# Reciprocals and spreading in halves behind the last P.V of an attention kernel, with the left-over tiles and the final stores placed anew

## The chip, the core and the metric

One core of a Trainium2 chip runs the whole kernel. The metric is the device time of one execution in microseconds (us), as the median of several runs.

## The reference

Sequence length S = 2048, model width D = 512, 32 heads of 16, hidden width F = 1792, all in fp32:

```python
xn  = layernorm(x)
qkv = xn @ wqkv                                # 32 heads of 16
p   = softmax(q @ k^T * 16 ** -0.5)            # full, per head
s   = (p @ v) @ wo                             # attention and its projection
g   = silu(relu(xn @ w1 + b1) ** 2 @ w2 + b2)  # feed-forward with squared relu
out = x + s * g
```

## The kernel before

The order of the work is written out by hand; every engine executes its own instructions in program order. Products of fp32 values are made with fp32r pairs: a value is split into a high and a low part (`h`, `l`), and a product is the sum of three matmuls (high.high, high.low, low.high); `group` issues these three.

A first part normalizes x and makes q, k and v. The middle, and nearly all of the time, is a loop of 64 turns (`TURNS`) over groups of four heads, chunks of 512 queries and halves of the keys. A turn makes scores for eight key blocks on TensorE, the exponentials on ScalarE (VectorE copies some scores out of PSUM first), and then the products P.V, which `values_of` issues one behind the other (line 850) into the PSUM bank `acc`. Between the score matmuls a turn also carries matmuls of the feed-forward part or, in the last turns, of the projection with `wo`. V carries a column of ones, so that P.V also yields the row sums of the softmax.

The output has 16 tiles of 128 rows, 4 for each chunk of queries. Tiles of chunks 0 and 1 are projected during the last turns. For the tiles of chunks 2 and 3, the last groups of heads are missing until the end: `rest(i, dst)` (i = 0 to 3) makes the left-over products for tile i of chunk 2, from the columns of `onorm[2, 3]`; `end_rest(i, src)` multiplies them with 0.5 and the gate and brings them to the output rows, by a DMA that accumulates onto rows that are stored already (issued by GpSimd), or, for i = 2, by an addition on GpSimd of rows loaded back before (`stored`) and a plain store. I call these the left-over tiles 0 to 3.

What follows the last P.V serves chunk 3. `ou` is the sum of the last two partial P.V results, with the 16 row sums (4 heads by 4 row blocks) in columns of their own. In order: transposing products with columns of the identity bring the row sums into PSUM (line 1193); a copy and a reciprocal (1195, 1197); products of a broadcast reciprocal with the identity spread them over `ou`'s layout (1200); `check` and three instructions (887 to 1206) fold the ranges of all row sums into one flag per partition, which a product with ones (1209) sums into `nvalid`; `ou` is normalized (1212) and split into `h` (ScalarE, 1213) and `l` (VectorE, 1215); four projections with `wlast`, the last rows of `wo`, give the four tiles of chunk 3; each is multiplied by 0.5 and the gate (1227), added to `base` (1229 on GpSimd for the first, 1232 on VectorE) and stored, by SP or ScalarE. The left-over tiles 2, 3 and 1 stand between these steps, 0 before the last P.V. At the end all engines load `nvalid` and skip `general_path`, which is for inputs outside the ranges; SP waits for the transfers' counters.

`wlast` is loaded in the turn before the last by `load_wlast`, four DMAs on SP's queue, and split by VectorE (`split_wlast`); `load_stored` is a DMA on GpSimd's queue half a turn later. PSUM is full all the time: two tiles of two banks for scores and one (`spare`, S0) for the side work, and the banks `acc` and `lin`; behind the last scores they become free (`two`, `small`).

Of the kernel before, what the change touches and what calls it, by code (L numbers as in the profile page):

```python
# [24 lines left out]
FT = mybir.dt.float32  # L25
FR = mybir.dt.float32r
I32 = mybir.dt.int32
AF = mybir.ActivationFunctionType
OP = mybir.AluOpType
AX = mybir.AxisListType  # L30
# [46 lines left out]
def fast_path(tc, sb, banks, env):  # L77
# [14 lines left out]
    def t(shape, dt, tag):  # L92

        cnt[0] += 1
        if tag in BUFS:
            turn[tag] = turn.get(tag, -1) + 1
            n = turn[tag] % BUFS[tag]
            p, tag = ps.get(tag), f"{tag}{places[n] if tag == 'S' else n}"
        else:
            p = None  # L100
        return (p or ps.get(tag, sb)).tile(shape, dt, tag=tag, name=f"{tag}_{cnt[0]}")
# [901 lines left out]
    def load_wlast():  # L1003
        wlast.append(t([128, 512], FT, "u"))
        pool.memset(wlast[0], 0.0)
        for j in range(4):
            sp.dma_start(wlast[0][32 * j:32 * j + 16], wo[448 + 16 * j:464 + 16 * j])

    def split_wlast():
        a = t([128, 2, 512], FR, "QA")  # L1010
# [48 lines left out]

    def load_stored():  # L1060

        stored.append(t([128, 512], FT, "hl0"))
        pool.dma_start(stored[0], out[1280:1408])

    at(LAST + 1, load_base3)
    at(LAST + 6.5, load_stored)
# [14 lines left out]
    def rest(i, dst):  # L1081

        group(dst, lambda p: onorm[2, 3][p][:, cut[i]], lambda p: wos[0][p][1][:, 1])

    def end_rest(i, src):

        o = t([128, 512], FT, f"wf2{'hl'[i // 2]}{i % 2}")
        dve.scalar_tensor_tensor(o, src, 0.5, gsb[2, i // 2][:, i % 2], op0=OP.mult, op1=OP.mult)
        rows = out[1024 + 128 * i:1152 + 128 * i]
        if i == 2:  # L1090
            pool.tensor_tensor(o, o, stored[0], op=OP.add)
            sp.dma_start(rows, o)
        else:
            pool.dma_start(rows, o, accum_op=OP.add)

    seen = t([1, 16], FT, "seen")

# [15 lines left out]
    for n in range(TURNS):  # L1113
# [43 lines left out]
            exps(*a)  # L1157
        if n == TURNS - 1:
            two = t([128, 2, 512], FT, "S")
            rest(0, two[:, 0])  # L1160
        pieces_now = pieces_of[n] if n < len(pieces_of) else 0
        ahead = pieces_now > 0 and n % per in (0, 1, 3, 6, 7, 10, 11)
        while lin(0, 1):
# [4 lines left out]
        if n == LAST + 4:  # L1168
            gsb.update({(1, i): y[1, i] for i in range(2)})
        if n == TURNS - 1:  # L1170
            end_rest(0, two[:, 0])
        happen(n + 0.5)
        for _ in range(pieces_now - ahead):
            split_piece()
# [3 lines left out]
        happen(time / 2)  # L1178


    ou = t([128, 512], FT, "P0")
    zc, r = t([128, 16], FT, "zc"), t([128, 16], FT, "rc")
    ok, okm, ones = t([128, 80], FT, "ok"), t([128, 1], FT, "okm"), t([128, 1], FT, "ones")
    dve.memset(ones, 1.0)
    h, l = t([128, 512], FR, "wf1h0"), t([128, 512], FR, "wf1l0")
    half = [slice(0, 256), slice(256, 512)]
    for s in half:
        dve.tensor_tensor(ou[:, s], sides[0][:, s], part[0][:, s], op=OP.add)
    small = t([128, 2, 512], FT, "S")
    lins = [small[:, 1], t([128, 512], FT, "lin"), t([128, 512], FT, "acc"), two[:, 0]]  # L1190
    rest(2, spare[:, 0])
    for i in range(4):
        mm(lins[1][:, 4 * i:4 * i + 4], ou[:, cut[i]], ident[:, 16::32], start=True, stop=True)
    end_rest(2, spare[:, 0])
    dve.tensor_copy(zc, lins[1][:, :16])
    rest(3, lins[2])
    dve.reciprocal(r, zc)
    for i in range(4):
        for j in range(4):
            mm(small[32 * j:32 * j + 32, 0, cut[i]], r[:, 4 * i + j:4 * i + j + 1].broadcast_to([128, 32]), ident,  # L1200
               start=True, stop=True)

    check(zc, 4 * NQ - 1)
    dve.tensor_scalar(ok[:, 0:32], stat[:, 0:32], Z_MIN, None, op0=OP.is_ge)
    dve.tensor_scalar(ok[:, 32:80], stat[:, 32:80], BIG, None, op0=OP.is_le)
    dve.tensor_reduce(okm, ok, axis=AX.X, op=OP.min)
    end_rest(3, lins[2])
    pn = spare[0:1, 1, :1]
    mm(pn, okm, ones, start=True, stop=True)
    rest(1, two[:, 1])  # L1210
    for s in half:
        dve.tensor_tensor(ou[:, s], small[:, 0, s], ou[:, s], op=OP.mult)
        act.copy(h[:, s], ou[:, s])
    for s in half:
        dve.tensor_tensor(l[:, s], ou[:, s], h[:, s].bitcast(FT), op=OP.subtract)
    dve.tensor_copy(nvalid, pn)
    end_rest(1, two[:, 1])


    o = [t([128, 512], FT, f"P{2 + i}") for i in range(4)]  # L1220
    for j in range(2):
        for todo in ((0, 0), (0, 1)), ((1, 0),):
            for i in (2 * j, 2 * j + 1):
                group(lins[i], lambda p: (h, l)[p][:, cut[i]], lambda p: wlast[0][:, p],
                      start=len(todo) == 2, stop=len(todo) == 1, todo=todo)
        for i in (2 * j, 2 * j + 1):
            dve.scalar_tensor_tensor(o[i], lins[i], 0.5, gsb[3, j][:, i % 2], op0=OP.mult, op1=OP.mult)
            if i == 0:
                pool.tensor_tensor(o[0], o[0], base[3, 0][:, 0], op=OP.add)
                act.dma_start(out[1536:1664], o[0])  # L1230
    for i, eng in ((1, sp), (2, act), (3, sp)):
        dve.tensor_tensor(o[i], o[i], base[3, i // 2][:, i % 2], op=OP.add)
        eng.dma_start(out[1536 + 128 * i:1664 + 128 * i], o[i])


def general_path(tc, dram, nvalid, ident, vdram, kdram, qdram, gdram, x, wo, out):
# [109 lines left out]
```

## Time and profile before

| | |
|---|---|
| three runs | 1212.72, 1213.26, 1214.46 us; median 1213.26 |
| the profiled execution: its own time | 1212.94 us |
| its span, first to last instruction | 1211.2 us |
| granted TensorE clock, mean | 0.998 |
| busy: TensorE, ScalarE, VectorE, GpSimd | 99%, 86%, 70%, 29% of the span |

In the profile PE is TensorE, DVE VectorE, ACT ScalarE, POOL GpSimd, SP SyncE; a q behind a name is the engine's queue, where DMAs are issued. A row of a timeline has start and duration in us, engine, line of the kernel, operation, output tile <- input tiles, shapes and count; where several instructions are merged, the duration is of all of them, and in brackets stands the idle time before and what ended it. Rows of a line's instructions have min/median/max of the duration in ns, first and last start, forms. Ends of matmuls are modelled.

### The profile page before, as it was taken

How to read it: one execution, taken by the hardware profiler on the slowest of the kernel's cores; microseconds unless marked ns; L12 is line 12 of the kernel's file. 1: busy time of each engine (PE TensorE's matmuls, PEld its weight loads, DVE VectorE, ACT ScalarE, POOL GpSimd, SP SyncE). 2: the span in 40 equal slices, each digit the busy share in tenths (PEclk: the TensorE clock that was granted, in tenths of full speed). 3: DMA queues.
4: the chain of work that ended last, by engine and by line, in shares of the span. 5: the costliest groups of instructions: out<-in, count | busy, mean ns of one | idle time of the engine just before them, and what ended most of it. 6: DMA issues, size and time to landing. Idle time of an engine off the chain costs nothing.

```text
span 1211.2 us, 24228 instructions
## 1 busy us (share of the span) xinstructions
PE 1200.1 (99%) x9877; PEld 709.9 (59%) x9877; DVE 845.4 (70%) x1365; ACT 1040.8 (86%) x1231; POOL 350.1 (29%) x268
## 2 busy tenths in 40 slices
PE   9999999999999999999999999999999999999996
PEld 7888655555565555555555565555555555555553
DVE  7666767575866776757687676677775758777776
ACT  6655689889989889988999988889898889999993
POOL 5756523040312321304032122221230404222222
PEclk9999999999999999999999999999999999999999
DMA  7799914131343222224423133151422233464444
GB/s 290 293 371 322 332 58 137 45 111 44 97 154 109 75 69 85 67 75 149 120 77 111 46 97 85 45 183 42 118 80 80 80 99 79 132 207 151 157 140 103
DMA packets 107576, 154.91 MB, mean 128 GB/s; under 512 B 43386, under 2 KB 57736, under 8 KB 107460
## 3 DMA queue, kind: packets, MB, share of 16 engines
q1 hardware_dynamic: 104804, 144.93, 37.3%
q0 software_dynamic: 2368, 7.87, 2.2%
q8 instruction: 78, 1.28, 0.4%
q10 hardware_dynamic: 288, 0.52, 0.1%
q14 instruction: 38, 0.31, 0.1%
HBM read 103.61 MB, written 49.67 MB: 127 GB/s over the span
## 4 chain that ended last, share of the span: by engine, by line
PE 97%; DVE 1%; DMA 1%; SPq 0%; issue 0%; ACT 0%; DVEq 0%
PE acc L850 36%; PE S L551 28%; PE S L503 14%; PE B L314 5%; PE acc L503 5%; PE B L127 4%; PE lin L503 2%; PE D L314 1%; PE D L252 1%; DMA hl<-gd 0%; PE S L993 0%; PE lin L314 0%; SPq L880 0%; PE acc L314 0%; DMA P<-in_A_x_dram 0%
## 5 line engine op out<-in xcount | busy, mean ns | idle before, releaser
L507 ACT ACTIVATE P<-S 128x1024 f32<-128x1024 f32 x702 | 661.9, 1040 | 93.7 <-PE S L503 91.9
L850 PE MATMUL acc<-P,V 128*32 128x512 f32 x4096 | 453.6, 594 | 0.0
L526 DVE COPY P<-acc 128x512 f32<-128x512 f32 x322 | 222.8, 692 | 139.7 <-PE lin L503 69.2
L507 ACT ACTIVATE P<-P 128x1024 f32<-128x1024 f32 x322 | 315.0, 1090 | 0.0
L850 PEld LDWEIGHTS acc<-P,V 128*32 128x32 f32 x4096 | 126.3, 110 | 285.6 <-issue 265.6
L503 PE MATMUL S<-QA,KA 64*128 64x512 f32 x1404 | 292.0, 405 | 0.0
L526 DVE COPY P<-lin 128x512 f32<-128x512 f32 x322 | 220.6, 685 | 1.5 <-PE lin L503 0.6
L503 PEld LDWEIGHTS S<-QA,KA 64*128 64x128 f32 x1404 | 134.6, 184 | 111.2 <-issue 41.8
L503 PE MATMUL lin<-QA,KA 64*128 64x512 f32 x322 | 126.8, 394 | 0.0
L503 PE MATMUL acc<-QA,KA 64*128 64x512 f32 x322 | 126.6, 393 | 0.1
L120 POOL TENSOR_TENSOR wf1l<-wr,wf1h 128x1024 fp32r<-128x1024 f32 x28 | 68.4, 2442 | 176.9 <-DVE wf1h L116 108.4
L577 POOL MEMSET note<- 1x1 f32 x68 | 6.0, 88 | 383.2 <-PE S L551 381.7
L551 PE MATMUL S<-xl,wf1h 64*128 64x512 f32 x464 | 95.8, 389 | 0.0
L120 POOL TENSOR_TENSOR hl<-T,hh 128x1024 fp32r<-128x1024 f32 x28 | 79.9, 2855 | 52.9 <-DVE hh L116 52.9
L120 POOL TENSOR_TENSOR wf2l<-wr,wf2h 128x1024 fp32r<-128x1024 f32 x28 | 67.2, 2401 | 90.5 <-DVE wf2h L116 90.5
L551 PE MATMUL S<-xh,wf1l 64*128 64x512 f32 x480 | 91.3, 388 | 0.0
L551 PE MATMUL S<-wf2l,hh 64*128 64x512 f32 x448 | 90.3, 390 | 0.0
L876 DVE TENSOR_TENSOR ou<-acc,ou 128x512 f32<-128x512 f32 x31 | 21.4, 692 | 96.8 <-PE acc L850 91.0
L551 PE MATMUL S<-wf2h,hl 64*128 64x512 f32 x448 | 82.9, 388 | 0.0
L551 PE MATMUL S<-xh,wf1h 64*128 64x512 f32 x480 | 77.7, 392 | 0.0
L551 PE MATMUL S<-wf2h,hh 64*128 64x512 f32 x448 | 71.7, 393 | 0.0
L503 PEld LDWEIGHTS acc<-QA,KA 64*128 64x128 f32 x322 | 59.3, 184 | 17.1 <-DVE P L526 2.4
(370 smaller groups left out, 1427.7 us busy)
## 6 DMA issues: line engine op xcount, KB each, us to landing
wr<-in_B_w_dram SPq DMA_DIRECT2D x56, 512.0 KB
QA<-qd SPq DMA_DIRECT2D x128, 128.0 KB
KA<-kd SPq DMA_DIRECT2D x64, 256.0 KB
u<-ud SPq DMA_DIRECT2D x15, 512.0 KB
kd<-P SPq DMA_DIRECT2D x11, 512.0 KB
V<-vd SPq DMA_DIRECT2D x8, 664.0 KB
qd<-P SPq DMA_DIRECT2D x9, 512.0 KB
vd<-P SPq DMA_DIRECT2D x16, 280.0 KB
```

Of the source, the lines that this page charges most:

```text
L120: leng.tensor_tensor(lo, src, hi.bitcast(FT), op=OP.subtract)
L127: mm(dst, lhs(a, k), rhs(b, k), start=n == 0, stop=n == len(todo) - 1)
L252: nc.tensor.transpose(halves[k // 2][:, k % 2, 128 * j:128 * j + 128], xnorm[c, i][:, j, 128 * k:128 * k + 128], ident)
L314: mm(dst, left[a][:, k], right[b][:, k], start=n == 0, stop=n == 5)
L503: mm(dst, k[r, p, 128 * (kb % 8):128 * (kb % 8) + 128], q[r, p], start=True, stop=True)
L507: act.activation(ptile[i, p], src, AF.Exp, scale=SCALE)
L526: dve.tensor_copy(ptile[i, p][:, hp], sides[hp])
L551: ins = mm(bank, self.lhs(a, k)[r], self.rhs(b, k)[r], start=n == 0 and self.at[other] == 0, stop=n == len(self.todo[half]) - 1 and self.a ...
L577: f = pool.memset(note[:, notes[0]:notes[0] + 1], 0.0)
L850: mm(sides[0][32 * j:32 * j + 32], vq[qd][:, kb, 17 * j:17 * j + 32], ptile[i, j // 2][:, j % 2], start=first, stop=last)
L876: dve.tensor_tensor(ou, sides[0], part[0], op=OP.add)
```

## The change

Both reciprocals and the spreading are done in two halves, for columns 0 to 255 and 256 to 511 of `ou`, each with a PSUM bank of its own, and the reciprocals read PSUM directly. The normalized values stay in PSUM (`norms`). The flag work of line 1204 to 1206 moves ahead of the additions; the last row sums are checked through the largest and smallest reciprocal (`top`, `flags`) instead of through `check`. Left-over tile 1 moves ahead of the last P.V, next to tile 0; tile 3's matmuls go between the spreading and the last projections; tile 2 is scaled by ScalarE and multiplied with its gate on GpSimd; tile 3 is added to loaded rows on GpSimd and stored by ScalarE in place of the accumulating DMA. In the final projections GpSimd adds `base` for tiles 0 and 1, VectorE for 2 and 3, with the multiplied values of these two left in PSUM; ScalarE issues all four stores, in the order 0, 2, 1, 3. Two of the four loads of `wlast` go to GpSimd's queue, and `load_stored` loads two tiles.

```diff
@@ -1004,7 +1004,7 @@
         wlast.append(t([128, 512], FT, "u"))
         pool.memset(wlast[0], 0.0)
         for j in range(4):
-            sp.dma_start(wlast[0][32 * j:32 * j + 16], wo[448 + 16 * j:464 + 16 * j])
+            (sp, pool)[j // 2].dma_start(wlast[0][32 * j:32 * j + 16], wo[448 + 16 * j:464 + 16 * j])
 
     def split_wlast():
         a = t([128, 2, 512], FR, "QA")
@@ -1059,8 +1059,8 @@
 
     def load_stored():
 
-        stored.append(t([128, 512], FT, "hl0"))
-        pool.dma_start(stored[0], out[1280:1408])
+        stored.append(t([128, 2, 512], FT, "hl0"))
+        pool.dma_start(stored[0], out[1280:1536].rearrange("(a p) d -> p a d", p=128))
 
     at(LAST + 1, load_base3)
     at(LAST + 6.5, load_stored)
@@ -1084,14 +1084,18 @@
 
     def end_rest(i, src):
 
-        o = t([128, 512], FT, f"wf2{'hl'[i // 2]}{i % 2}")
-        dve.scalar_tensor_tensor(o, src, 0.5, gsb[2, i // 2][:, i % 2], op0=OP.mult, op1=OP.mult)
+        o, gate = t([128, 512], FT, f"wf2{'hl'[i // 2]}{i % 2}"), gsb[2, i // 2][:, i % 2]
+        if i == 2:
+            act.activation(o, src, AF.Copy, scale=0.5)
+            pool.tensor_tensor(o, o, gate, op=OP.mult)
+        else:
+            dve.scalar_tensor_tensor(o, src, 0.5, gate, op0=OP.mult, op1=OP.mult)
         rows = out[1024 + 128 * i:1152 + 128 * i]
-        if i == 2:
-            pool.tensor_tensor(o, o, stored[0], op=OP.add)
-            sp.dma_start(rows, o)
+        if i < 2:
+            pool.dma_start(rows, o, accum_op=OP.add)
         else:
-            pool.dma_start(rows, o, accum_op=OP.add)
+            pool.tensor_tensor(o, o, stored[0][:, i - 2], op=OP.add)
+            (sp, act)[i - 2].dma_start(rows, o)
 
     seen = t([1, 16], FT, "seen")
 
@@ -1157,7 +1161,8 @@
             exps(*a)
         if n == TURNS - 1:
             two = t([128, 2, 512], FT, "S")
-            rest(0, two[:, 0])
+            for m in range(2):
+                rest(m, two[:, m])
         pieces_now = pieces_of[n] if n < len(pieces_of) else 0
         ahead = pieces_now > 0 and n % per in (0, 1, 3, 6, 7, 10, 11)
         while lin(0, 1):
@@ -1168,7 +1173,8 @@
         if n == LAST + 4:
             gsb.update({(1, i): y[1, i] for i in range(2)})
         if n == TURNS - 1:
-            end_rest(0, two[:, 0])
+            for m in range(2):
+                end_rest(m, two[:, m])
         happen(n + 0.5)
         for _ in range(pieces_now - ahead):
             split_piece()
@@ -1178,59 +1184,64 @@
         happen(time / 2)
 
 
+    ok, okm, flags = t([128, 80], FT, "ok"), t([128, 1], FT, "okm"), t([128, 2], FT, "ones")
+    dve.tensor_scalar(ok[:, 0:32], stat[:, 0:32], Z_MIN, None, op0=OP.is_ge)
+    dve.tensor_scalar(ok[:, 32:80], stat[:, 32:80], BIG, None, op0=OP.is_le)
+    dve.tensor_reduce(okm, ok, axis=AX.X, op=OP.min)
+
     ou = t([128, 512], FT, "P0")
-    zc, r = t([128, 16], FT, "zc"), t([128, 16], FT, "rc")
-    ok, okm, ones = t([128, 80], FT, "ok"), t([128, 1], FT, "okm"), t([128, 1], FT, "ones")
-    dve.memset(ones, 1.0)
+    r = t([128, 16], FT, "rc")
     h, l = t([128, 512], FR, "wf1h0"), t([128, 512], FR, "wf1l0")
     half = [slice(0, 256), slice(256, 512)]
     for s in half:
         dve.tensor_tensor(ou[:, s], sides[0][:, s], part[0][:, s], op=OP.add)
+    rest(2, spare[:, 0])
+    end_rest(2, spare[:, 0])
     small = t([128, 2, 512], FT, "S")
-    lins = [small[:, 1], t([128, 512], FT, "lin"), t([128, 512], FT, "acc"), two[:, 0]]
-    rest(2, spare[:, 0])
-    for i in range(4):
-        mm(lins[1][:, 4 * i:4 * i + 4], ou[:, cut[i]], ident[:, 16::32], start=True, stop=True)
-    end_rest(2, spare[:, 0])
-    dve.tensor_copy(zc, lins[1][:, :16])
-    rest(3, lins[2])
-    dve.reciprocal(r, zc)
-    for i in range(4):
-        for j in range(4):
-            mm(small[32 * j:32 * j + 32, 0, cut[i]], r[:, 4 * i + j:4 * i + j + 1].broadcast_to([128, 32]), ident,
-               start=True, stop=True)
-
-    check(zc, 4 * NQ - 1)
-    dve.tensor_scalar(ok[:, 0:32], stat[:, 0:32], Z_MIN, None, op0=OP.is_ge)
-    dve.tensor_scalar(ok[:, 32:80], stat[:, 32:80], BIG, None, op0=OP.is_le)
-    dve.tensor_reduce(okm, ok, axis=AX.X, op=OP.min)
-    end_rest(3, lins[2])
-    pn = spare[0:1, 1, :1]
-    mm(pn, okm, ones, start=True, stop=True)
-    rest(1, two[:, 1])
-    for s in half:
-        dve.tensor_tensor(ou[:, s], small[:, 0, s], ou[:, s], op=OP.mult)
-        act.copy(h[:, s], ou[:, s])
-    for s in half:
-        dve.tensor_tensor(l[:, s], ou[:, s], h[:, s].bitcast(FT), op=OP.subtract)
+    lin, acc = t([128, 512], FT, "lin"), t([128, 512], FT, "acc")
+    for n, z in enumerate((lin, acc)):
+        for i in range(2):
+            mm(z[:, 4 * i:4 * i + 4], ou[:, cut[2 * n + i]], ident[:, 16::32], start=True, stop=True)
+        dve.reciprocal(r[:, 8 * n:8 * n + 8], z[:, :8])
+    top = [two[:, 0, n:n + 1] for n in range(2)]
+    dve.tensor_reduce(top[0], r, axis=AX.X, op=OP.max)
+    dve.tensor_reduce(top[1], r, axis=AX.X, op=OP.min)
+    norms = [small[:, 0, :256], spare[:, 1, :256]]
+    for n in range(2):
+        for i in range(2):
+            for j in range(4):
+                k = 8 * n + 4 * i + j
+                mm(norms[n][32 * j:32 * j + 32, cut[i]], r[:, k:k + 1].broadcast_to([128, 32]), ident,
+                   start=True, stop=True)
+    dve.tensor_tensor(norms[0], norms[0], ou[:, half[0]], op=OP.mult)
+    dve.scalar_tensor_tensor(flags[:, 0:1], top[0], 1 / Z_MIN, okm, op0=OP.is_le, op1=OP.mult)
+    dve.tensor_scalar(flags[:, 1:2], top[1], 1 / BIG, None, op0=OP.is_ge)
+    dve.tensor_tensor(norms[1], norms[1], ou[:, half[1]], op=OP.mult)
+    for n, s in enumerate(half):
+        act.copy(h[:, s], norms[n])
+    for n, s in enumerate(half):
+        dve.tensor_tensor(l[:, s], norms[n], h[:, s].bitcast(FT), op=OP.subtract)
+    rest(3, lin)
+    pn = acc[0:1, :1]
+    mm(pn, flags[:, 0:1], flags[:, 1:2], start=True, stop=True)
+    end_rest(3, lin)
     dve.tensor_copy(nvalid, pn)
-    end_rest(1, two[:, 1])
-
-
-    o = [t([128, 512], FT, f"P{2 + i}") for i in range(4)]
+
+
+    o, lins = [t([128, 512], FT, f"P{2 + i}") for i in range(4)], [two[:, 0], small[:, 1], acc, lin]
     for j in range(2):
         for todo in ((0, 0), (0, 1)), ((1, 0),):
             for i in (2 * j, 2 * j + 1):
                 group(lins[i], lambda p: (h, l)[p][:, cut[i]], lambda p: wlast[0][:, p],
                       start=len(todo) == 2, stop=len(todo) == 1, todo=todo)
         for i in (2 * j, 2 * j + 1):
-            dve.scalar_tensor_tensor(o[i], lins[i], 0.5, gsb[3, j][:, i % 2], op0=OP.mult, op1=OP.mult)
-            if i == 0:
-                pool.tensor_tensor(o[0], o[0], base[3, 0][:, 0], op=OP.add)
-                act.dma_start(out[1536:1664], o[0])
-    for i, eng in ((1, sp), (2, act), (3, sp)):
-        dve.tensor_tensor(o[i], o[i], base[3, i // 2][:, i % 2], op=OP.add)
-        eng.dma_start(out[1536 + 128 * i:1664 + 128 * i], o[i])
+            dve.scalar_tensor_tensor(lins[i] if j else o[i], lins[i], 0.5, gsb[3, j][:, i % 2], op0=OP.mult, op1=OP.mult)
+            if j == 0:
+                pool.tensor_tensor(o[i], o[i], base[3, 0][:, i], op=OP.add)
+    for i in (2, 3):
+        dve.tensor_tensor(o[i], lins[i], base[3, 1][:, i % 2], op=OP.add)
+    for i in (0, 2, 1, 3):
+        act.dma_start(out[1536 + 128 * i:1664 + 128 * i], o[i])
 
 
 def general_path(tc, dram, nvalid, ident, vdram, kdram, qdram, gdram, x, wo, out):
```

## The prediction, made before the change was run

> **What bounds the kernel now.** I read the page first, then the chain of waits for the last 30 us, then the timeline of that stretch engine by engine, then the DMA view of two short windows and the instructions of a few lines. Times in these views are us from the start of the span.
>
> ```profile
> span 1211.2 us, 24228 instructions
> ```
>
> From the chain of waits (start, duration, engine, tile, line):
>
> ```profile
> 1187.14 7.00 PE acc L850 x64
> 1194.14 0.90 PE S L993 x3
> ...
> 1198.55 0.41 ACT wf1h L1213
> 1198.96 0.04 issue
> 1199.01 0.73 PE S L993 x2
> ...
> 1204.25 0.68 DVE P L1232
> ```
>
> Up to the last P.V (L850, which ends at about 1194.1) TensorE carries the chain without a gap. Behind it the chain goes back and forth between VectorE, ScalarE and TensorE, and the last addition of VectorE ends at 1204.93. The change touches this last 17 us of the 1211.2 and little else, so no large share of the time is at stake. The timeline of TensorE and of VectorE there:
>
> ```profile
> 1186.51 0.40 PE L993 MATMUL S<-xl,hl 128*128 128x512 f32 x1
> 1186.75 0.39 PE L993 MATMUL S<-xh,hl 128*128 128x512 f32 x1
> 1187.07 7.07 PE L850 MATMUL acc<-P,V 128*32 128x512 f32 x64
> ...
> 1194.88 0.95 PE L1193 MATMUL lin<-ident,P 128*128 128x4 f32 x8
> ...
> 1196.56 1.08 PE L1200 MATMUL S<-ident,rc 128*32 128x128 f32 x32
> 1197.64 0.19 PE L1209 MATMUL S<-ones,okm 128*1 128x1 f32 x2
> 1197.76 0.50 PE L993 MATMUL S<-xh,hl 128*128 128x512 f32 x1
> ```
>
> ```profile
> 1194.29 0.75 DVE L1188 TENSOR_TENSOR P<-acc,ou 128x256 f32<-128x256 f32 x2 [2.88 <-PE acc L850]
> ...
> 1195.87 0.17 DVE L1195 COPY zc<-lin 128x16 f32<-128x16 f32 x1
> 1196.08 0.25 DVE L1197 RECIPROCAL rc<-zc 128x16 f32<-128x16 f32 x1
> 1196.24 0.11 DVE L887 TENSOR_REDUCE stat<-zc 128x1 f32<-128x16 f32 x1
> 1196.27 0.15 DVE L888 TENSOR_REDUCE stat<-zc 128x1 f32<-128x16 f32 x1
> 1196.39 0.83 DVE L1204 TENSOR_SCALAR ok<-stat 128x32 f32<-128x32 f32 x1
> 1197.14 0.17 DVE L1205 TENSOR_SCALAR ok<-stat 128x48 f32<-128x48 f32 x1
> 1197.35 0.23 DVE L1206 TENSOR_REDUCE okm<-ok 128x1 f32<-128x80 f32 x1
> 1197.50 0.68 DVE L1088 SCALAR_TENSOR_TENSOR wf2l<-acc,V 128x512 f32<-128x512 f32 x1
> 1198.10 0.74 DVE L1212 TENSOR_TENSOR P<-S,P 128x256 f32<-128x256 f32 x2
> ...
> 1200.47 0.69 DVE L1227 SCALAR_TENSOR_TENSOR P<-S,wr 128x512 f32<-128x512 f32 x1
> ```
>
> Two things are to be seen. VectorE has the flag work (L887 to L1206) and one left-over tile (L1088) between its reciprocal and the normalisation L1212, although the spread values (L1200) are ready at 1197.64 and would be earlier. And the first comparison, L1204, takes 0.83 for 32 columns where its twin takes 0.17 for 48: it ends at 1197.22, as soon as GpSimd's addition does (1195.91 + 1.28, first row here):
>
> ```profile
> 1195.91 1.28 POOL L1091 TENSOR_TENSOR wf2l<-wf2l,hl 128x512 f32<-128x512 f32 x1 [4.72 <-issue]
> 1198.49 0.89 POOL L1094 DMA_DIRECT2D out_dram<-wf2l  x1 [1.31 <-DVE wf2l L1088]
> 1200.70 0.85 POOL L1094 DMA_DIRECT2D out_dram<-wf2h  x1 [1.32 <-DVE wf2h L1088]
> 1201.31 1.53 POOL L1229 TENSOR_TENSOR P<-P,KA 128x512 f32<-128x512 f32 x1
> ```
>
> The stores, issued by SP and by ScalarE, and what the DMA moved in 40 slices of 1197 to 1200 (0.075 us each) and of 1202 to 1212 (0.25 us each):
>
> ```profile
> 1197.21 0.36 SPq L1092 DMA_DIRECT2D out_dram<-wf2l  x1
> 1203.75 1.54 SPq L1233 DMA_DIRECT2D out_dram<-P  x2
> ```
>
> ```profile
> 1202.87 0.38 ACTq L1230 DMA_DIRECT2D out_dram<-P  x1
> 1204.36 0.57 ACTq L1233 DMA_DIRECT2D out_dram<-P  x1
> ```
>
> ```profile
> GB/s 0 0 0 0 0 0 0 0 0 0 0 0 0 0 191 410 437 410 437 437 382 410 273 110 0 0 0 0 0 0 0 0 0 0 0 0 0 0 0 191
> ```
>
> ```profile
> GB/s 74 98 16 90 49 172 188 197 197 123 311 393 377 377 377 418 401 385 393 377 213 90 57 33 25 25 0 0 0 0 33 0 0 0 0 0 0 0 0 0
> ```
>
> A store of 256 KB alone (issued 1197.21) has its data moved by 1198.8, 1.6 us after its issue. The last of the kernel (the second of the SP pair, issued at about 1204.96, right behind VectorE's end at 1204.93) has its data moved only by 1208.5, 3.5 us after: up to 1204.5 the DMA moves the two accumulating stores of GpSimd (1198.49 and 1200.70) at 200 GB/s or less, so the final stores queue up. Then the exit: SP reads eight counters off, one after the other, before it passes to the end.
>
> ```profile
> L1246 SPq EVENT_SEMAPHORE  x8: 17/17/17, 1209.0 to 1209.5; - x8
> ```
>
> **The change, part by part.** Times are put on the clock of the profile before, and the shift of the first part is added at the end.
>
> *Left-over tile 1 ahead of the last P.V.* Three more matmuls on TensorE at 0.24 each (1186.51 to 1186.75), in front of an unbroken chain: +0.7. Their multiplication on VectorE (0.68), the two comparisons and the reduction (0.17, 0.17, 0.23; 0.83 if one has to wait for GpSimd) fall into the 2.88 that VectorE idles during the P.V, so they cost nothing; without that cover they would cost 1.3 to 1.9. Its accumulating store is issued some 10 us earlier and moves during the P.V; on GpSimd's queue nothing waits behind it.
>
> *Behind the P.V.* Left-over tile 2's matmuls and the additions L1188 stay. The eight matmuls of L1193 now fill two banks: the first four end at about 1195.4, so the first reciprocal (0.25 at most, the row has 16 columns) is done by 1195.7, the second by 1196.1; the copy zc (0.21 of the chain) goes. The spreading (1.08 for 32) starts when TensorE is through with L1193, 1195.8 for 1196.56, and gives its halves at 1196.4 and 1196.9. VectorE has two short reductions before (0.26), then the first normalisation half at 1196.45, two flag instructions on one column (0.1 to 0.15 each, by the reductions), the second half at about 1197.05. ScalarE's first copy starts at 1196.9 for 1198.55.
>
> TensorE then becomes the late one: left-over tile 3 (0.9 like the row at 1194.14, 1196.85 to 1197.75 including its start) and the flag product stand in front of the last projection. Between products of 128 and of 32 or fewer columns the rows show 0.32 from one start to the next (1186.75 to the P.V at 1187.07) where 0.24 is usual, and 0.12 from the flag product to the next (1197.64 to 1197.76). That puts the projection at 1197.8 to 1197.9 for 1199.01, and with the unchanged 1.46 to the first L1227 (1199.01 to 1200.47), that instruction at 1199.3 for 1200.47: -1.2. With the +0.7 it is -0.5.
>
> *From the first L1227 to the last issue.* Before: seven VectorE instructions, 4.49 to the last issue at 1204.96. After: VectorE has six (0.6 a step, 3.9 to the end of the last, PSUM as a source and target being taken like SBUF), but GpSimd has five operations from 1195.8 on: ScalarE's scaled copy ends at about 1195.7
>
> ```profile
> L259 ACT COPY V<-D x1: 607/607/607, 14.9 to 14.9; 128x512 f32<-128x512 f32 x1
> ```
>
> (0.61 behind tile 2's product, which ends at about 1195.05), then multiplication and addition for tile 2 (to 1198.4 or 1198.9, at 1.28 and 1.53), the addition for tile 3 once VectorE has delivered it at about 1198.95, and the two base additions. With 1.4 each, between the two rows, the last ends at 1203.2, against 1203.2 on VectorE: they are level. ScalarE issues all four final stores in the order 0, 2, 1, 3; what is queued behind its wait for GpSimd's tile 1 is store 3, which goes 0.4 to 0.57 later (the two ACT rows): 1203.7, so 1204.4 with the +0.7, for 1204.96: -0.55. The bounds are 1204.1 and 1204.9 with 1.28 and 1.53 throughout.
>
> *Landing.* No accumulating store is left in the way. The last store follows store 1 on the same queue: data from 0.85 after store 1's issue at 0.65 to 0.75 per store (410 to 437 GB/s on one queue, in the window at 1197), 1.9 after its own issue. Before, the transfers of the last store also thin out for 1 us (from 213 down to 25 GB/s): a few of the 16 engines are behind. I keep 0.6 of that: 2.5 for 3.5, so -1.0; bounds 1.9 and 3.5. The Trainium skill, "DMA: Bandwidth & Descriptors", section on the anatomy of one DMA, has about 2.0 us plus bytes over 436 GB/s, an estimate of 2.6 for 256 KB, and its fit is for GpSimd's path; by it the undisturbed store would take 1.0 more than the 1.6 seen here until its data are through, part of which is the receipt that this row does not hold, and the sum would hardly gain here.
>
> *Exit.* Of the eight waits the first holds SP until 1209.0, so the last store's counter is read first and the seven others follow at 0.07. The counters are taken in turn by the transfers of SP and ScalarE; the change takes two away (half of wlast's loads) and adds one (tile 3's store), which by my count moves the last store to the eighth place: -0.45, or nothing if they are not given out in turn.
>
> *Loads that move.* Two of the four wlast loads go to GpSimd's queue, and the load of the stored rows doubles.
>
> ```profile
> 1164.95 1.76 SPq L1007 DMA_DIRECT2D u<-in_A_wo_dram  x4
> L116 DVE CAST QA<-u x1: 618/618/618, 1173.4 to 1173.4; 128x512 fp32r<-128x512 f32 x1
> ```
>
> The split that uses wlast runs at 1173.4, 6.7 after the last issue, and the stored rows are wanted some 20 us after their load: nothing. If that cover failed, VectorE would hold up the score copies by what is missing.
>
> Sum: +0.7 - 1.2 (-0.5), -0.05 to the last issue, -1.0, -0.45: **-2.0**. The profiled run took 1212.94 (1211.2 and 1.7 around it), 0.3 below the median of 1213.26; from the median, 1211.2.
>
> **Rivals.** (a) *The tail comes out short*: GpSimd at 1.28 (-0.3), the flag product costs no pause (-0.2), no engine is behind in the DMA (-0.6): -3.1, 1210.1. For it speaks the clean transfer at 1197; against it, that two GpSimd rows differ by 0.25 for one shape.
> (b) *The late landing stays*: the thinning from 213 to 25 GB/s comes from something other than the accumulating stores, and the single queue adds its own wait: -1.0 in all, 1212.2.
> (c) *The flag comparison waits for GpSimd as L1204 did*: it stands ahead of the second normalisation half, and GpSimd works without a pause from 1195.8 to 1198.4: +1.3, in all -0.7, 1212.5. Against it: comparisons from PSUM do not stretch beside GpSimd's additions, all 56 within 9 ns:
>
> ```profile
> L627 DVE TENSOR_SCALAR T<-S,b1t x56: 740/745/749, 147.7 to 1024.0; 128x512 f32<-128x512 f32 x56
> ```
>
> The Trainium skill, "SBUF — State Buffer", section "Who interferes with whom", counts tensor_scalar among the operations that can take the port pair shared with GpSimd, whole instruction against whole instruction; L1204 agrees with 0.83, L627 does not show it for a source in PSUM, which is where the new comparison reads.
> (d) *Slower: ScalarE's queue*. Five stores of 256 KB (tile 3's and the final four) go through it from about 1202 on; before it never had more than two, and never alone. Its rate decides: below 186 GB/s (1.31 MB in the 7.0 us until 1208.95) the new end is later than the old. At 123 GB/s, the lowest slice of the mixed stretch after 1203.5, it needs 10.6 us: +3.6, 1216.9. Against it: SP's queue alone reaches 437.
> (e) *GpSimd last*: at 1.9 for each of its five operations the new end equals the old; the slowest row here has 1.53.
>
> **How the numbers follow.** About 0.2%, 2.4 us, is what a measurement of this kernel can tell from no change. Forecast 52% (own range 1210.4 to 1212.0, a quarter of it below 1210.8), (a) 21%, (b) 14%, (c) 6%, (d) 4%, (e) 3%. Faster by over 0.2%: 0.21 + 0.13 = 0.34; slower by over 0.2%: 0.05, (d) and a little of what I have not seen; the rest, 0.61, within it. The runs shown lie between 0.5 below and 1.2 above their median, so the range runs from 0.5 below (a), 1209.6, to 1.1 past (c), 1213.6.
>
> **What would show it.** Right: the last P.V ends 0.7 later; the first multiplication of the final projection at 1200.0 on the new clock; no 0.83 comparison behind the P.V; last issue, on ScalarE, at 1204.4; data through at about 1206.9; SP's last wait of the eight, not its first, is the long one. Wrong: the P.V not later, the second normalisation half over 0.5 behind the first, GpSimd's base additions ending more than 0.5 behind VectorE, or slices below 300 GB/s after 1204 with data still moving at 1208.

## The result and the profile after

The kernel after takes 1211.62 us (median of 22 runs, 1210.83 to 1213.69), the kernel before 1213.66 in the runs beside it (22 runs, 1212.48 to 1215.15): the medians differ by 2.0 us. The ratio is 0.9986 with a 95% interval of 0.998 to 0.9992, which is 1.7 us less, between 1.0 and 2.4.

```profile
span 1211.2 us, 24241 instructions
```

The profiled span equals that of before, because this one execution reached the tail 2.0 us later. Over the fourteen profiles of this document the tail begins between 1185.37 and 1188.16, so one span says little about the tail. All places below are counted from the start of left-over tile 0's product, which is 1186.18 in the trace of before and 1188.16 in that of after. TensorE in the kernel after (start, duration, engine, line, operation, tiles):

```profile
1188.16 0.50 PE L993 MATMUL S<-xh,hl 128*128 128x512 f32 x1
1188.50 0.40 PE L993 MATMUL S<-xl,hl 128*128 128x512 f32 x1
1188.74 0.62 PE L993 MATMUL S<-xh,hl 128*128 128x512 f32 x2
...
1189.75 7.07 PE L850 MATMUL acc<-P,V 128*32 128x512 f32 x64
...
1198.43 1.10 PE L1214 MATMUL S<-ident,rc 128*32 128x128 f32 x32
1199.47 0.50 PE L993 MATMUL lin<-xh,hl 128*128 128x512 f32 x1
...
1200.36 0.19 PE L1226 MATMUL acc<-ones 128*1 128x1 f32 x2
1200.48 1.20 PE L993 MATMUL S<-QA,wf1h 128*128 128x512 f32 x4
```

Two left-over tiles now stand ahead of the P.V, which begins 1.59 behind the first of them, where it was 0.89. The last projection begins at 12.32, where it was 12.83 (1199.01). VectorE there:

```profile
1193.88 0.17 DVE L1188 TENSOR_SCALAR ok<-stat 128x32 f32<-128x32 f32 x1
1194.00 0.19 DVE L1189 TENSOR_SCALAR ok<-stat 128x48 f32<-128x48 f32 x1
1194.23 0.24 DVE L1190 TENSOR_REDUCE okm<-ok 128x1 f32<-128x80 f32 x1
1196.96 0.75 DVE L1197 TENSOR_TENSOR P<-acc,ou 128x256 f32<-128x256 f32 x2 [2.50 <-PE acc L850]
...
1199.22 0.43 DVE L1216 TENSOR_TENSOR S<-S,P 128x256 f32<-128x256 f32 x1
1199.56 0.15 DVE L1217 SCALAR_TENSOR_TENSOR ones<-S,okm 128x1 f32<-128x1 f32 x1
1199.62 0.15 DVE L1218 TENSOR_SCALAR ones<-S 128x1 f32<-128x1 f32 x1
1199.69 0.42 DVE L1219 TENSOR_TENSOR S<-S,P 128x256 f32<-128x256 f32 x1
...
1201.94 1.29 DVE L1238 SCALAR_TENSOR_TENSOR P<-S,wr 128x512 f32<-128x512 f32 x2 [0.32 <-PE S L993]
...
1205.12 0.68 DVE L1242 TENSOR_TENSOR P<-lin,KA 128x512 f32<-128x512 f32 x1
```

The flag work L1188 to L1190 lies in the wait for the P.V, and the comparison that took 0.83 takes 0.17. The two normalisation halves (L1216, L1219) start 0.47 apart. The first final multiplication is at 13.78 (before: 14.29). GpSimd and the issues of ScalarE:

```profile
1198.48 1.26 POOL L1090 TENSOR_TENSOR wf2l<-wf2l,V 128x512 f32<-128x512 f32 x1 [4.34 <-ACT wf2l L1089]
1199.83 1.29 POOL L1097 TENSOR_TENSOR wf2l<-wf2l,hl 128x512 f32<-128x512 f32 x1
1201.65 1.30 POOL L1097 TENSOR_TENSOR wf2l<-wf2l,hl 128x512 f32<-128x512 f32 x1 [0.53 <-DVE nvalid L1228]
1202.91 2.50 POOL L1240 TENSOR_TENSOR P<-P,KA 128x512 f32<-128x512 f32 x2
```

```profile
1202.98 0.38 ACTq L1098 DMA_DIRECT2D out_dram<-wf2l  x1
1204.21 2.81 ACTq L1244 DMA_DIRECT2D out_dram<-P  x4
```

GpSimd ends at 17.24 and VectorE at 17.63, but the last of the four issues starts at 18.43 only (0.34, 0.50, 0.68 and 0.42 long). The way out, from SP's branch and its eight counters:

```profile
L1257 SPq EVENT_SEMAPHORE  x8: 17/17/17, 1205.1 to 1209.5; - x8
L1257 SPq COMPARE_BRANCH  x1: 45/45/45, 1202.4 to 1202.4; - x1
```

The last store lands (the last of its completions is counted) at 1209.53, 21.37, and the last counter is passed then: the eighth is now the long one. The last instruction of the span starts at 23.02 (before: 24.96); this is called the end below.

### The profile page after: what moved, and what is told of

Its sections match the earlier page's. It is cut to its first block, busy times and chain, and to the rows that moved or that the text cites. A ratio compares the mean times of both kernels' runs of the same rounds, so it can differ in the third digit from the quotient of the medians.

```text
span 1211.2 us, 24241 instructions
## 1 busy us (share of the span) xinstructions
PE 1200.8 (99%) x9877; PEld 711.6 (59%) x9877; DVE 843.8 (70%) x1364; ACT 1041.1 (86%) x1232; POOL 354.5 (29%) x272
## 3 DMA queue, kind: packets, MB, share of 16 engines
q10 hardware_dynamic: 720, 1.31, 0.3%
## 4 chain that ended last, share of the span: by engine, by line
PE 95%; issue 2%; DVE 1%; POOL 1%; DMA 0%; SPq 0%; ACT 0%; DVEq 0%; POOLq 0%; ACTq 0%
PE acc L850 36%; PE S L551 28%; PE S L503 14%; PE acc L503 5%; PE B L314 4%; PE B L127 3%; PE lin L503 1%; POOL P L120 1%; PE B L681 1%; DMA hl<-gd 0%; PE D L314 0%; PE D L252 0%; PE S L993 0%; SPq L880 0%; PE lin L314 0%
```

## The experiments

Kernels that differ from after by one or two edits, or from before by parts of the change. Places are us from the start of tile 0's product, in one profiled run each; the ratio is to the kernel before beside it, with its 95% interval.

| kernel | first final mult. | VectorE's end | last issue, engine | last landing | end | ratio |
|---|---|---|---|---|---|---|
| before | 14.29 | 18.76 | 18.78 SP | 22.69 | 24.96 | |
| after | 13.78 | 17.63 | 18.43 ScalarE | 21.37 | 23.02 | 0.9986 (0.998, 0.9992) |
| e0_after (after again) | 13.79 | 17.63 | 18.46 ScalarE | 21.46 | 23.13 | 0.9984 (0.9975, 0.9993) |
| e1_two_queues | 13.78 | 17.64 | 17.66 SP | 21.29 | 24.00 | 0.9995 (0.9986, 1.0004) |
| e2_flag_late | 13.46 | 17.30 | 17.33 SP | 20.47 | 24.09 | 0.9999 (0.999, 1.0008) |
| e3_wlast_sp | 13.80 | 17.65 | 18.01 ScalarE | 21.11 | 23.21 | 0.9991 (0.9982, 1.0) |
| e4_before_tile1_early | 15.02 | 19.49 | 19.52 SP | 22.51 | 25.35 | 1.0003 (0.9994, 1.0012) |
| e5_accum3 | 13.78 | 17.63 | 18.86 ScalarE | 21.76 | 23.49 | 0.9992 (0.9983, 1.0001) |
| e6_flags_sbuf | 13.78 | 17.65 | 18.01 ScalarE | 21.09 | 22.75 | 0.9985 (0.9976, 0.9995) |
| e7_flag_between | 13.47 | 17.65 | 18.74 ScalarE | 21.70 | 23.37 | 0.9985 (0.9976, 0.9994) |
| e8_sp_first | 13.78 | 17.64 | 18.09 ScalarE | 21.64 | 23.29 | 0.9991 (0.9982, 1.0) |
| e9_before_act | 14.30 | 18.75 | 19.84 ScalarE | 22.92 | 25.10 | 1.0001 (0.9992, 1.001) |
| e10_before_flags | 13.93 | 18.38 | 18.41 SP | 21.83 | 24.46 | 0.9996 (0.9987, 1.0005) |
| e11_but_halves | 14.61 | 19.09 | 19.12 ScalarE | 22.07 | 24.26 | 0.9996 (0.9987, 1.0005) |

Differences of half a us between two kernels are within these intervals (each about 1.1 us to either side), so what follows is read from the places, and the times only say that the tail as a whole is right.

### The end: who issues the last store

e0_after, the same kernel again: 

> The changed kernel once more, beside the others of this set. Times in the tail are counted from the start of left-over tile 0's product. Both theories: 0.9982 to 0.9986 of the kernel before; tail 23.0 us for 25.0; last store issued at 18.4, landed at 21.4.

It gives the spread of one profile against another: up to 0.03 to the last issue, 0.11 at the end.

e1_two_queues:

```diff
-    for i in (0, 2, 1, 3):
-        act.dma_start(out[1536 + 128 * i:1664 + 128 * i], o[i])
+    for i, eng in ((0, act), (2, sp), (1, act), (3, sp)):
+        eng.dma_start(out[1536 + 128 * i:1664 + 128 * i], o[i])
```

> The changed kernel with stores 0 and 1 issued by ScalarE, 2 and 3 by SP. Theory A (ScalarE's own issuing, 0.34 to 0.68 us a store, makes the last store 0.8 us later than VectorE's last addition): last issue at 17.7 for 18.4, within 0.05 of VectorE's end, tail 22.3 to 22.5, time 0.5 to 0.7 us under e0_after. Theory B (the DMA engines' rate sets the landing, whichever queue the stores wait in): issue earlier by 0.7, landing not, tail 22.9 to 23.1, same time as e0_after.

The last issue comes 0.80 earlier than in e0_after and the end 0.87 later. SP's rows in e1_two_queues:

```profile
L1257 SPq EVENT_SEMAPHORE  x8: 17/17/17, 1208.4 to 1208.9; - x8
L1257 SPq COMPARE_BRANCH  x1: 50/50/50, 1205.6 to 1205.6; - x1
```

in e0_after:

```profile
L1257 SPq EVENT_SEMAPHORE  x8: 17/17/17, 1203.7 to 1208.1; - x8
L1257 SPq COMPARE_BRANCH  x1: 50/50/50, 1201.0 to 1201.0; - x1
```

and in before:

```profile
L1246 SPq EVENT_SEMAPHORE  x8: 17/17/17, 1209.0 to 1209.5; - x8
L1246 SPq COMPARE_BRANCH  x1: 45/45/45, 1206.4 to 1206.4; - x1
```

From the branch to the first counter SP needs 2.8, 2.8 and 2.6. In e1_two_queues all had landed by 1207.85 and SP still passed the first counter only at 1208.37. SP branches behind its own last issue; where ScalarE issues the last store, SP branches early and these 2.6 to 2.8 lie beside the stores. In before the two came together: landing at 22.69, first counter at 22.79. To see which held it there, a part of the change was put into before by itself.

e10_before_flags: L1204 to L1206 of before go to the place behind the last P.V's start, and the check of the last row sums is left out.

```diff
+    dve.tensor_scalar(ok[:, 0:32], stat[:, 0:32], Z_MIN, None, op0=OP.is_ge)
+    dve.tensor_scalar(ok[:, 32:80], stat[:, 32:80], BIG, None, op0=OP.is_le)
+    dve.tensor_reduce(okm, ok, axis=AX.X, op=OP.min)
     ou = t([128, 512], FT, "P0")
...
-    check(zc, 4 * NQ - 1)
-    dve.tensor_scalar(ok[:, 0:32], stat[:, 0:32], Z_MIN, None, op0=OP.is_ge)
-    dve.tensor_scalar(ok[:, 32:80], stat[:, 32:80], BIG, None, op0=OP.is_le)
-    dve.tensor_reduce(okm, ok, axis=AX.X, op=OP.min)
```

> The kernel before, with the two comparisons of the stored statistics and their reduction moved ahead of the two additions, behind the last P.V's start; the check of the last row sums is left out. Theory (VectorE's queue holds the first normalisation in the kernel before: the comparisons lie behind the reciprocal and ahead of the third left-over tile's multiplication): first final multiplication 0.3 to 0.5 earlier, 13.8 to 14.0 in place of 14.29, last issue and SyncE's way out as much earlier; the end 0 to 0.4 earlier, since the last landing holds it too; time 0 to 0.4 us below before. Rival (TensorE's 16 spreading products set the normalisation): first final multiplication stays at 14.2 to 14.3.

The last landing is 0.86 earlier than in before, the end only 0.50, and the first counter passes 0.47 after the last landing:

```profile
L1245 SPq EVENT_SEMAPHORE  x8: 17/17/17, 1209.1 to 1209.6; - x8
L1245 SPq COMPARE_BRANCH  x1: 45/45/45, 1206.5 to 1206.5; - x1
```

The 0.50 is what SP's branch gained (19.67 for 20.18). Where SP does wait for the last landing (nine of these profiles, after among them), the counter passes 0.02 behind it; in before it passed 0.10 behind, 2.6 after the branch. So SP's own way was the end of before, by a hair, and an earlier landing alone is worth nothing there. e4_before_tile1_early, below, says the same: landing 0.18 earlier, end 0.39 later. The other half alone is e9_before_act:

```diff
-    for i, eng in ((1, sp), (2, act), (3, sp)):
+    for i, eng in ((1, act), (2, act), (3, act)):
```

> The kernel before, with one edit: ScalarE issues all four final stores (before: 0 and 2 ScalarE, 1 and 3 SyncE). Theory (in the kernel before SyncE's way out and the last landing came at the same moment, 22.79 and 22.69, so that either alone gains little): ScalarE's last issue 18.8 to 19.2, the last landing stays near 22.5 to 22.8 because the accumulating store of left-over tile 1 is still issued at 14.5; SyncE's way out is hidden; the end is the landing and 1.65 to 2.1, 24.2 to 24.8 in place of 24.96; time 0.2 to 0.7 us below before. Rival 1 (SyncE's way out alone was the end): end at about 23.0 and time 2 us below. Rival 2 (the issuing engine means nothing for the end): end 24.96 as before, or later by what ScalarE's queue costs (0.2 to 0.4).

SP branches at 1201.3 there and its first counter passes at 1209.3, with the last landing (22.92, 1209.30). But ScalarE's issues took 1.42, 0.65 and 0.41 in place of 0.34 (from the first to the end of the third 2.68), so that the last began at 19.84. The 0.2 to 0.7 expected did not come; rival 2 describes the end (25.10, 0.14 later), though not for its reason. Neither an earlier landing nor SP's early branch gains by itself; together they do, as e11_but_halves below and after show.

e3_wlast_sp puts the four wlast loads on SP again, which shifts the last store's counter from the eighth place to the second.

```diff
-            (sp, pool)[j // 2].dma_start(wlast[0][32 * j:32 * j + 16], wo[448 + 16 * j:464 + 16 * j])
+            sp.dma_start(wlast[0][32 * j:32 * j + 16], wo[448 + 16 * j:464 + 16 * j])
```

> The changed kernel with all four wlast loads on SP's queue again. Theory A (transfers of SP and ScalarE take eight completion counters in turn, SP reads them off in order, 0.067 each): the last store's counter comes to the second place instead of the eighth, landing unchanged, exit from the last landing to the end 2.05 for 1.65, time 0.4 above e0_after. Rival (the exit does not depend on it): exit 1.65, same time.

From landing to end: 2.10, for 1.65 to 1.67 in after and e0_after; 2.18 in e9_before_act and 2.19 in e11_but_halves, where the first counter is the long one. The place of the counter is worth 0.07 to 0.08 a step, near the forecast.

e8_sp_first gives SP only the first of the four:

```diff
-    for i in (0, 2, 1, 3):
-        act.dma_start(out[1536 + 128 * i:1664 + 128 * i], o[i])
+    for i, eng in ((0, sp), (2, act), (1, act), (3, act)):
+        eng.dma_start(out[1536 + 128 * i:1664 + 128 * i], o[i])
```

> The kernel after, with one edit: SyncE issues store 0, ScalarE the other three (2, 1, 3). Counted from the start of left-over tile 0's product. Theory (SyncE's way out starts behind its last issue and takes some 5.8 to 6.3 us to the end; ScalarE's queue of four sets the last issue in the kernel after): SyncE issues store 0 at 16.05, its way out would be over by 21.9 to 22.4 and so stays hidden; ScalarE, rid of one issue, issues store 3 at 17.8 to 18.1 in place of 18.43, last landing 20.9 to 21.1 in place of 21.4, end 22.6 to 23.0 in place of 23.0 to 23.1; time 0 to 0.4 us below that of the kernel after, too little for the runs to tell. Rival (any issue by SyncE behind the last product is on the way out): end at 23.3 or above, as with the two queues (24.0).

SP branched at 1204.4 and had its first counter at 1207.1, 1.9 before the last landing (1209.0): hidden, as the theory says. The end at 23.29 is the rival's number, but by another way: ScalarE's three issues took 0.34, 0.48 and 0.75, and the last store landed 3.55 after its issue.

### The middle: which part moves the first final multiplication

e4_before_tile1_early is before with left-over tile 1 ahead of the last P.V:

```diff
-            rest(0, two[:, 0])
+            for m in range(2):
+                rest(m, two[:, m])
...
-            end_rest(0, two[:, 0])
+            for m in range(2):
+                end_rest(m, two[:, m])
...
-    rest(1, two[:, 1])
...
-    end_rest(1, two[:, 1])
```

> The kernel before with one part of the change alone: left-over tile 1 ahead of the last P.V, its accumulating store with it; SP still issues the last store. Times from the start of tile 0's product. Theory C (the way out is SP's own: last store issued, flag loaded, branch, 2.6 to 2.8 us after the branch until the first counter is read, then twenty waits at 0.066; 6.2 us from SP's last issue to the end): P.V 0.7 later, last issue at 19.3 to 19.5 for 18.8, landing earlier than 22.7 but the end later, 25.5 to 25.7 for 25.0; 0.6 us slower than before. Theory D (the landing of the last store is what the exit waits for, as forecast): landing at 21.4 to 22.0, end at 23.7 to 24.3, 0.7 to 1.3 us faster than before.

The P.V moves by 0.70 and the first final multiplication by 0.73, from 14.29 to 15.02: tile 1's old place behind the P.V had cost that multiplication nothing. e11_but_halves is e4_before_tile1_early with the edits of e10_before_flags and e9_before_act:

> The kernel before, with all the parts of the change but the halves and GpSimd's additions: left-over tile 1 ahead of the last P.V, the comparisons ahead of the additions (the check of the last row sums left out), all four final stores by ScalarE. Theory: P.V 0.69 later; first final multiplication 15.02 less 0.3 to 0.5, so 14.5 to 14.7; VectorE's end 19.0 to 19.2; ScalarE's last issue 19.0 to 19.5; last landing 2.9 behind it, 21.9 to 22.4; end 1.65 to 2.1 behind that, 23.6 to 24.5, against 23.0 to 23.1 of the kernel after; time 0.5 to 1.4 us above the kernel after, 0.5 to 1.4 below before. The difference of 0.7 to 0.9 at the first final multiplication is then what the halves alone bring. Rival (the halves bring nothing, the gain is all order and issue): first final multiplication at 13.8 and end at 23.1, as in the kernel after.

So at the first final multiplication: tile 1 +0.73, the comparisons with the check left out -0.41 (-0.36 in e10_before_flags), the rest -0.83 (14.61 to 13.78), in all -0.51. The forecast numbers all came. But the rest is not the halves alone, as the expectation has it: e11_but_halves also keeps the row sums' copy and the old places of tiles 2 and 3, whose multiplications (0.69 each on VectorE) and tile 3's products on TensorE still stand ahead of the normalisation. No run parts these from the halves. The rows of VectorE in e11_but_halves show what it waits for:

```profile
1195.96 0.25 DVE L1202 RECIPROCAL rc<-zc 128x16 f32<-128x16 f32 x1
1196.57 0.69 DVE L1088 SCALAR_TENSOR_TENSOR wf2l<-acc,V 128x512 f32<-128x512 f32 x1 [0.35 <-PE acc L993]
1197.61 0.76 DVE L1212 TENSOR_TENSOR P<-S,P 128x256 f32<-128x256 f32 x2 [0.35 <-PE S L1210]
```

VectorE has free time now (0.35 ahead of L1212) and waits for the spreading of all 16 columns, which ends on TensorE at 1197.54 with the flag product L1210 right behind it; the normalisation starts at 12.23 there and at 11.06 in after. Of the gain by VectorE's end, 1.46 (19.09 to 17.63), the other 0.63 is the addition of tile 1, which GpSimd makes instead (tile 0's it made before).

Three edits of after tried the flag work. e6_flags_sbuf:

```diff
-    top = [two[:, 0, n:n + 1] for n in range(2)]
+    top = [t([128, 1], FT, f"top{n}") for n in range(2)]
```

> The changed kernel with the largest and the smallest reciprocal in SBUF tiles instead of PSUM. Theory (a comparison from SBUF to SBUF waits for GpSimd's addition to end, as L1204 did; from PSUM it does not): the comparison on the smallest takes 0.8 to 1.3 instead of 0.15, the second normalisation half starts 0.7 to 1.2 later, the first final multiplication at 14.3 to 14.9 for 13.8. Rival (one column is too short to take the shared pair): 0.1 to 0.2, nothing later.

```profile
1197.99 0.14 DVE L1218 TENSOR_SCALAR ones<-top 128x1 f32<-128x1 f32 x1
1198.06 0.42 DVE L1219 TENSOR_TENSOR S<-S,P 128x256 f32<-128x256 f32 x1
```

The comparison from SBUF takes 0.14, not 0.83. That doesn't settle the point: GpSimd's first operation there ended at 1198.05 and its second began at 1198.13 (1.29, the row of L1097), so that the comparison fell on the gap between the two. The end, 22.75, is the earliest of all, because ScalarE's issues took 0.34 to 0.41 in that run; the time is that of after.

e2_flag_late is e1_two_queues with the flag product behind the final projections:

```diff
     rest(3, lin)
-    pn = acc[0:1, :1]
-    mm(pn, flags[:, 0:1], flags[:, 1:2], start=True, stop=True)
     end_rest(3, lin)
-    dve.tensor_copy(nvalid, pn)
...
+    pn = spare[0:1, 0, :1]
+    mm(pn, flags[:, 0:1], flags[:, 1:2], start=True, stop=True)
     for i in (2, 3):
         dve.tensor_tensor(o[i], lins[i], base[3, 1][:, i % 2], op=OP.add)
+    dve.tensor_copy(nvalid, pn)
```

> As e1_two_queues, and the flag product with its copy to nvalid moved from ahead of the final projections to behind them. Theory A (TensorE's order, with a pause of 0.32 plus 0.12 around the one-column product, is what the projections wait for, ScalarE's high part being ready 0.4 earlier): first projection at 11.9 for 12.3, first multiplication at 13.35 for 13.8, VectorE's end 0.4 earlier, tail 0.3 to 0.5 shorter than e1's; GpSimd's last base addition then ends last. Rival (the projections wait for the high part, or VectorE is full before): under 0.1 us in each place.

```profile
1199.07 0.39 PE L993 MATMUL lin<-xh,hl 128*128 128x512 f32 x1
1199.30 1.08 PE L993 MATMUL S<-QA,wf1h 128*128 128x512 f32 x4
```

The first four projection products follow tile 3 after 0.23, where in after the flag product made it 0.44 (1200.04 to 1200.48). VectorE ends 0.33 earlier, yet the end is no earlier than in e1_two_queues: SP's first counter passed 3.4 after its branch (1205.7 to 1209.1), with all landed at 1207.66. The flag did not hold SP's branch: it was ready at 1204.55, and SP loaded it at 1204.90, right behind its last issue, as in e1_two_queues. What differs is that all five engines branch together, between 1205.43 and 1205.72.

e7_flag_between puts the flag product between the two pairs of projections, and store 0 on SP. 

> The changed kernel with the flag product between the first and second pair of final projections, its copy to nvalid behind the second final multiplication, and store 0 issued by SP, 2, 1 and 3 by ScalarE. Theory C: the first final multiplication at 13.45 (as in e2), VectorE's end at 17.4, last issue at 17.6 to 17.9, SP through its branch by 17.5, so the exit waits for the landing at 20.6 to 20.9; end 22.2 to 22.6, 0.5 to 0.8 us faster than e0_after. Against it (something else in e2 made its end late, not the late flag): end above 23.3.

```profile
1200.94 0.14 DVE L1242 CAST nvalid<-S 1x1 int32<-1x1 f32 x1
1201.44 0.70 DVE L1238 SCALAR_TENSOR_TENSOR acc<-acc,wr 128x512 f32<-128x512 f32 x1 [0.35 <-PE acc L993]
```

The first multiplication comes 0.31 earlier, but the second pair of projections is now 0.35 late for VectorE, which ends at 17.65 as before: the product has to be paid for in one of the two places. Nothing is gained. The end, 23.37, misses the 22.2 to 22.6 expected: ScalarE's issue of store 1 took 1.13, so that the last issue came at 18.74.

### The landing

e5_accum3 gives tile 3 its accumulating store back:

```diff
-        if i < 2:
+        if i != 2:
             pool.dma_start(rows, o, accum_op=OP.add)
```

> The changed kernel with left-over tile 3 brought to its rows by an accumulating store of GpSimd again, in place of GpSimd's addition and ScalarE's store. Theory: the accumulating store moves its data at 200 GB/s or less while the final stores queue up, so the last landing comes 3.4 to 3.9 after the last issue for 2.9 to 3.0; GpSimd ends 0.3 to 0.5 earlier, ScalarE has a store less; time 0.2 to 0.8 above e0_after. Rival (accumulating stores do not hold the others up): 2.9 from issue to landing, time 0.3 under e0_after.

From issue to landing the last store takes 2.90, as in after (2.93): it has not become slower. What moved is the issue: ScalarE's four stretch over 3.69, for 2.81 in after, and two of them took 1.27 and 0.75.

```profile
1203.21 3.69 ACTq L1244 DMA_DIRECT2D out_dram<-P  x4
```

```profile
q0 software_dynamic: 144, 0.26, 50.8%
q10 hardware_dynamic: 244, 0.46, 31.3%
```

In the window from 1202 to 1206 the accumulating store (q0) takes half the time of the 16 engines for 0.26 MB, the plain stores (q10) a third for 0.46. The two long issues began at 1204.79, when the accumulating store was about to end (1204.83) and a fetch of 16 KB of instructions was moving (1204.69 to 1205.70), and at 1206.15, 0.45 behind that fetch; which of the two made them long is not shown. In e11_but_halves the accumulating store was over at 1201.2, and ScalarE's three issues, ready one after the other, took 0.34 each:

```profile
1203.29 1.54 ACTq L1232 DMA_DIRECT2D out_dram<-P  x3
```

As to the landing itself e5_accum3 decides nothing: its accumulating store was over 1.32 before the last issue. In before one was still moving behind the last issue (the window from 1204.96 to 1207; packets, MB, share of the 16 engines' time):

```profile
q0 software_dynamic: 7, 0.01, 3.4%
```

Its last packet ended 0.99 behind the last issue there, 0.49 in e10_before_flags and 0.15 in e9_before_act, and the last store landed 3.91, 3.42 and 3.08 behind its issue: in all three 2.92 to 2.93 behind that packet. e4_before_tile1_early is before with that one accumulating store out of the way, the same issuers and the same 0.60 between the issues: 2.99 (one profile each). So in before the accumulating store did make the landing late, by 0.9. It is not the only thing that can: e1_two_queues and e8_sp_first have none near the end, and 3.63 and 3.55; their cause is open.

## Why the prediction was right, point by point

- *Tile 1 ahead of the P.V*: +0.7 forecast, +0.69 found, its work on VectorE hidden in the wait for the P.V.
- *Behind the P.V*: forecast for the first copy, the last projection and the first L1227 (the new L1238), on the clock of before and without the +0.7, were 1196.9, 1197.8 to 1197.9 and 1199.3; found 1197.0, 1197.8 and 1199.3. Net -0.51 for -0.5. One of its reasons, that VectorE's flag work held the normalisation, carries a third of it (0.41 of 1.24); the halves, and tiles 2 and 3 out of the way, carry the rest together.
- *Rival (c)* did not come: the second half follows the first after 0.47. In after the first of the two flag instructions, with its column in PSUM, lay inside a GpSimd operation (1198.48 to 1199.74) and took 0.15; a comparison from SBUF across one was not tried in the new place.
- *To the last issue*: the forecast was 1204.4 on the clock of before, found 18.43, that is 1204.61; -0.35 for -0.55 against before. VectorE took 3.85 (forecast 3.9), and GpSimd's five operations 1.25 to 1.30 where 1.4 was taken. Rival (a) counted on such a GpSimd for 0.3, but ScalarE's issues ended later and hid it. **The mis-sized term is ScalarE's issue**: 0.50 and 0.68 for stores 2 and 1, where up to 0.57 for the one ahead of store 3 was allowed. In e3_wlast_sp and e6_flags_sbuf store 3 was issued at 18.01.
- *Landing*: 2.5 from the last issue to the end of the data was forecast; the data records end at 1209.09, 2.49 after the issue, for 3.57 before. To the landing 2.93, for 3.91: -0.98 for -1.0. Rival (b) fell. The accumulating store named as the cause is confirmed by e4_before_tile1_early (2.99), e9_before_act and e10_before_flags; it moved until 1205.95, longer than the 1204.5 that the working read.
- *Exit*: -0.45 forecast, -0.62 found (2.27 to 1.65). The counter's place gives 0.43 to 0.54 of it. **The reading of before was wrong here**: that its first counter passed with the last landing was taken as proof that SP waited for the landing. SP came there on its own, 0.10 behind the landing. The -1.0 and -0.45 were earned only because the last stores went to ScalarE at the same time, a condition that the working did not name. With SP issuing the last store (e1_two_queues) the issue comes 1.12 earlier than in before, and from there to the end it takes 6.34, for 6.18 in before and 4.59 in after: the two terms bring nothing, and 0.87 of the 1.8 to 1.9 is lost again. That the sum came out is to this extent luck.
- *Sum*: -1.94 and -1.83 in the two profiles of after, -2.0 between the medians, -1.7 (1.0 to 2.4) by the ratio; forecast -2.0. *Rival (d)*: ScalarE's queue moved its five stores, 1.31 MB, between 1203.87 and 1209.09, 251 GB/s with the pauses, above the 186 that decided.

## What to carry to other kernels

When two things end a kernel at the same moment, each hides what the other costs: move one alone and little comes of it, so look behind the last wait for the second in line before the gain is booked. Have the engine that walks the exit (SP here) issue its last transfer early, and let another engine issue the late ones. An accumulating store that still moves when the last store is issued makes that store land late (0.9 here). And count an issue of a transfer as work of its engine, with a length that is not constant (0.34 to 1.42 here).

## What was not expected of the hardware

- SP's way from its branch to the first counter takes 2.5 to 2.8 even with nothing left to land for that counter, 3.4 in e2_flag_late. In each profile a transfer of 8 KB of instructions (q14) begins 0.9 to 1.2 behind SP's branch, and where no landing holds the first counter, this passes 1.0 to 1.4 after that transfer's end; in e2_flag_late 1.9, with two more such transfers at its side and one of 16 KB behind it, until 1208.15. That SP waits for its instructions there is argued from these times, not shown. With SP issuing the last store the end came 5.8 to 6.8 after that issue (e4_before_tile1_early 5.8, e10_before_flags 6.1, before 6.2, e1_two_queues 6.3, e2_flag_late 6.8).
- The Trainium skill, "DMA: Bandwidth & Descriptors", section "Issuing engines are not separate DMA queues", says in effect that spreading transfers over engines does not add bandwidth. The runs agree as far as they go (landing 21.29 with two issuers, 21.37 to 21.46 with one), but the choice of the issuer moved the end by 0.9, by way of the exit.
- A 256 KB store takes 0.34 to issue, and up to 1.42 (e9_before_act). The long ones began while an accumulating store (219 to 249 ns a packet in the DMA records, for 75 to 79 of plain ones) or the fetch of 16 KB of instructions (1.0 to 2.5 long) was moving or within 0.5 of its end; in e11_but_halves, with both over by 1202.72, the three that follow are 0.34. That is a coincidence in time over these kernels; not every issue at such a time was long (0.34 at 1204.21 in after and at 1204.64 in e10_before_flags), and no run took the fetch away, so its part is not shown.
